# Linear attention and a gated feed-forward block on one core: group 1's output stage by seven block products, with the plan around it set anew

## The chip, the core and the metric

The kernel runs on one core of a Trainium2 chip. A core has five engines that run side by side and meet at semaphores: TensorE (PE; its weight loads are shown apart as PEld), VectorE (DVE), ScalarE (ACT), GpSimd (POOL) and SyncE (SP). DMAs are issued by SP, ACT or POOL. The metric is the device time of one execution in microseconds (us); of several executions the median counts.

## What is computed

```python
# q, k, v: [8 batches, 8 heads, 576 positions, 64]; cos_w, sin_w by position
def phi(x, c, s):
    r = np.maximum(x, 0.0)
    return np.concatenate([r * c, r * s], axis=-1)
kv  = einsum('bhsf,bhsd->bhfd', phi(k), v)
z   = sum(phi(k), axis=2)
x   = einsum('bhsf,bhfd->bhsd', phi(q), kv) / (einsum('bhsf,bhf->bhs', phi(q), z) + 1e-6)
x   = x.transpose(0, 2, 1, 3).reshape(4608, 512)          # tokens by model width
g   = x @ w_gate                                          # w_gate, w_val: [512, 1536]
out = (g * sigmoid(g) * (x @ w_val)) @ w_out              # w_out: [1536, 512], all float32
```

## The kernel before

**Tiles, groups, slots.** The 4608 tokens are 36 tiles of 128, and 9 groups (`tg` 0 to 8) of four tiles. A group's feed-forward work has twelve blocks (`fc`) of 128 hidden columns: gate and value products (`ffn_mm`, L605), silu on ACT (L611), product of the two on DVE into `ht` (L616). Then comes an output stage: `ht` times `w_out` for four tiles. While group `tg` runs, the attention of the next group's tiles is computed in between.

The order of all work is written out by hand. `slot(n)` is called 16 times per group (`SLOTS`, 12 after the blocks and 4 in the output stage) and runs what `plan` holds for slot n: so slot 16 tg + i is place i of group tg. The tables at the top set the places: `ROW[b]` for batch b those of `phi_q` (relu on ACT, L277, times cos/sin on DVE, L294, into `r_q`), of the DMA transposes of `r_q` into `phit` (L323, on SP's queue), of relu of k and of `vmul` (DVE, L304), and of the `kv` product (L354) with its copies out (L380 or L386); `TILES[tg]` those of the attention tiles (`a_tile2`: product L485, then `x_of` on DVE: L499, L508, L512, then `x_turn`, a DMA transpose into `xT` on SP's queue, L589). `WSUM` places four sums of gate weights (L638).

**Products by seven.** Groups 5 to 8 (`GATE`) compute the gate, and groups 2 to 8 the output, by a Strassen-like scheme: the matrices are cut into 2 x 2 blocks, and seven block products with sums of blocks (`ffn_by_quarters`, L663 for the gate and L676 for the value; `out_by_quarters`, L839) stand for eight. The output stage needs sums of weight blocks T1 to T4 (`weight_sum`, L802, kept in `wt_sb`) and of token blocks S1 to S4 (`token_sum`, L811, called by `sums_behind` after blocks 7 to 11, and inside the stage). The seven products are 12 matmuls of 256 columns each, in the order a, e = S3 T3, b += S2 T2, a again, b += S1 T1, c, b += S4. Between them: ACT copies a to b (L861) and e to C22 (L864), DVE adds C22 to c (L869) and b to C22 (L880), ACT copies out C11 and C21 (L852), DVE C12 (L854). Groups 0 and 1 multiply directly (`ffn_out`, L780: per tile twelve matmuls of 512 columns, then one copy, L787 on ACT or L789 on DVE). The weight sums are made inside group 1's output stage, one after each tile.

**PSUM banks.** `take` gives the eight banks in order of last use. From group 5 on (`loose`) it goes by `used`, an estimate of when a bank's reader will be done, and takes the earliest; `KVONE` lists the batches whose kv takes two single banks instead of a neighbouring pair.

**Loads and stores.** q, k and v of a batch (576 KB of float32 each, cast on the way) are loaded on GpSimd's queue. `load_behind(b)` first waits with a tiny copy (`hold`, L1051) until `phit` of batch b - 1 has landed. With `AHEAD = 5` it loads for b = 3: q3; for 4: q4, k4, v4, q5; for 5: k5, v5, q6; for 6: k6, v6, q7; for 7: k7, v7. Output rows are collected in `ob` and stored by `store` (L762, per tile two stores of 64 rows), in groups 1 to 7 on GpSimd's queue; the last group stores half-columns of two tiles by `store_two` (L769) and of one by `store`, one half of the rows from SP and the other from ACT.

Of the kernel before, what the change touches and what calls it, by code (L numbers as in the profile page):

```python
# [18 lines left out]
def kernel(  # L19
# [10 lines left out]
    nc = tc.nc  # L30
# [19 lines left out]
    HD = d_model // 2  # L50
    KH = KC // 2
    GATE = (5, 6, 7, 8)
    AHEAD = 5
    WSUM = (29, 38, 48, 64)
    ROW = {2: ([16, 16, 17, 17], 18, (20, 21, 21, 22), 8), 3: ([12, 12, 13, 13], 18, (17, 20, 21, 21), 6), 4: ([12, 12, 14, 14], 14, (13, 16, 17, 18), 5), 5: ([12, 12, 12, 14], 14, (14, 16, 17, 17), 5), 6: ([6, 8, 11, 12], 12, (13, 14, 15, 18), 3), 7: ([6, 6, 7, 7, 8, 8, 9, 9, 10, 10, 11, 11, 12, 12, 13, 13, 14, 14], 16, (12, 13, 14, 15), 3)}
    TILES = {2: (2, 9, 10, 11), 3: (5, 8, 10, 11), 4: (5, 7, 9, 11), 5: (3, 4, 7, 9), 6: (0, 2, 5, 7), 7: (0, 1, 5, 7), 8: (0, 3, 5, 7)}
    KVONE = (2, 5)
    LATER = {2: (0, 1, 3, 4, 7, 8), 3: (0, 1, 3, 4, 7, 8), 4: (0, 1, 3, 4, 7, 8), 5: (0, 1, 3, 4, 7, 8), 6: (0, 1, 3, 4, 7, 8), 7: (0, 1, 3, 4, 7, 8), 8: (0, 1, 3, 4, 7, 8)}
    LATE = dict(M=44, V=87, O=131, X=26, x=150, v=(190, 250, 120, 150), e=130, a=90, c=170, b=110, k=120)

# [21 lines left out]

    filled = [False] * 8
    loose = [False]
    rows = [0]

    def take(n, hold=None, fills=False, seeded=False):

        taken = {x for r in held.values() for x in r}
        if loose[0]:  # L90
            free = [b for b in range(8) if b not in taken]
            if n == 1:
                bs = [min((b for b in free if filled[b] or not seeded), key=lambda b: used[b])]
            else:
                b0 = min((b for b in free if b + 1 in free), key=lambda b: max(used[b:b + 2]))
                bs = [b0, b0 + 1]
            if hold is not None:
                held[hold] = bs
            for b in bs:
                filled[b] = fills or seeded  # L100
            touch(bs)
            return banks[:, bs[0]] if n == 1 else banks[:, bs[0]:bs[0] + 2]
        free = [b for b in range(0, 8, n) if not any(b <= x < b + n for x in taken)
                and (filled[b] or not seeded)]

        b0 = min(free, key=lambda b: (n == 1 and hold is not None and hold[0] == "o" and b ^ 1 not in taken,
                                      sorted(used[b:b + n], reverse=True)))
        if hold is not None:
            held[hold] = range(b0, b0 + n)
# [655 lines left out]
    def store_two(t, cols):  # L765
        for e in range(2):
            (b, c), (b1, _) = divmod(2 * t + e, NC), divmod(2 * t + 2 + e, NC)
            assert b == b1
            (nc.sync, nc.scalar)[e].dma_start(  # L769
                out=out_v[b, c:c + 3:2, :, cols].rearrange("c p f -> p c f"),  # L770
                in_=obs[t // 2][e * SH:(e + 1) * SH, :, cols])

# [40 lines left out]
    def sums_behind(fc):  # L813
        for n, lo, hi in {7: ((3, 0, 4),), 8: ((1, 0, 4),), 9: ((2, 0, 4),), 10: ((4, 0, 4), (3, 4, 6)),
                          11: ((1, 4, 6), (2, 4, 6))}.get(fc, ()):
            token_sum(n, lo, hi)

    def out_by_quarters(tg, slot_of):

        last = tg == NTG - 1  # L820
        queues = (nc.gpsimd, nc.gpsimd) if tg > 0 else None
        t0 = tg * OUT
        for t in (t0, t0 + 2):
            ob_of(t)
        C11, C12 = (obs[t0 // 2][:, :, x * HD:(x + 1) * HD] for x in range(2))
        C21, C22 = (obs[t0 // 2 + 1][:, :, x * HD:(x + 1) * HD] for x in range(2))

        def home(nm, parts=1, **kw):
            return [take(1, ("o", tg, nm, i), **kw).rearrange("p (t x) -> p t x", x=HD) for i in range(parts)]

        def free(nm, parts=1):
            for i in range(parts):
                give_back(("o", tg, nm, i))

        def product(to, a, b, first):
            rows[0] += LATE["O"]
            for kc in range(HC):
                for i in range(2):
                    nc.tensor.matmul(out=to[i][:, 0] if len(to) == 2 else to[0][:, i],  # L839
                                     lhsT=a[:, kc, i * P:(i + 1) * P], rhs=b[:, kc],  # L840
                                     start=first and kc == 0 and i == 0,
                                     stop=kc == HC - 1, skip_group_check=True)

        def each(ps, *others):
            if len(ps) == 1:
                return [(ps[0], *others)]
            return [(ps[i][:, 0:1], *(o[:, i:i + 1] for o in others)) for i in range(2)]

        def copied(eng, o, ps, x=DOWN):
            for p_, o_ in each(ps, o):  # L850
                if eng == "act":
                    nc.scalar.mul(out=o_, in_=p_, mul=x)  # L852
                else:
                    nc.vector.tensor_single_scalar(out=o_, in_=p_, scalar=x, op=ALU.mult)  # L854

        nb = 2 if last else 1
        a = home("a", fills=True)
        product(a, aq[:, 0, 0], bq[:, 0, 0], True)
        b = home("b", nb, seeded=True)
        for p_, o_ in each(b, a[0]):  # L860
            nc.scalar.copy(out=p_, in_=o_)  # L861
        e = home("e", fills=True)
        product(e, S3, T3, True)
        nc.scalar.mul(out=C22, in_=e[0], mul=DOWN)  # L864
        c = home("c", seeded=True)
        free("e")
# [12 lines left out]
        for p_, x_ in each(b, C22):  # L879
            nc.vector.scalar_tensor_tensor(out=x_, in0=p_, scalar=DOWN, in1=x_, op0=ALU.mult, op1=ALU.add)  # L880
        if last:
            store_two(t0 + 2, slice(HD, d_model))
        product(c, aq[:, 1, 1], T4, False)
        copied("act", C21, c)
        free("c")
        if last:
            store_two(t0 + 2, slice(0, HD))
        else:
            for t in (t0 + 2, t0 + 3):
                store(t, queues=queues)  # L890
        slot_of(2)
        product(b, S4, bq[:, 1, 1], False)
        copied("dve", C12, b)
        free("b", nb)
        for t in (t0, t0 + 1):
            store(t, *((slice(HD, d_model), (nc.sync, nc.scalar)) if last else (slice(0, d_model), queues)))
        slot_of(3)
# [41 lines left out]
    def turn(t, fast=False):  # L939
        return lambda: x_turn(t, fast)  # L940
# [83 lines left out]
    def load_2():  # L1024

        nc.gpsimd.tensor_copy(out=hold2, in_=xT[1][0:1, 0, 0, 0:2])
        for nm in ("k", "v"):
            load(2, nm)

    at((0, 1), turn(4), load_2)  # L1030
    at((1, 0), turn(5), a_(6, 0))
    at((1, 1), a_(6, 1))
# [70 lines left out]
    for tg in range(1, NTG):  # L1103
        s0 = SLOTS * tg
        if tg in GATE:
            if not loose[0]:
                loose[0] = True
                rows[0] = max(used) + 1
            ffn_by_quarters(tg, lambda i: slot(s0 + i))
        for fc in range(FC) if tg not in GATE else ():  # L1110
            ffn_fc(tg, fc)
            if tg > 1:
                sums_behind(fc)
            slot(s0 + fc)
        if tg > 1:
            out_by_quarters(tg, lambda i: slot(s0 + FC + i))
            continue
        for i in range(OUT):
            ffn_out(tg * OUT + i, queues=(nc.gpsimd, nc.gpsimd))
            weight_sum(i)  # L1120
            slot(s0 + FC + i)
    assert not plan, sorted(plan)


# [28 lines left out]
```

## Time and profile before

| | us |
|---|---|
| median of 4 runs (314.13 to 314.38) | 314.37 |
| the profiled execution | 314.13 |
| its span, first to last instruction | 312.3 |
| PE busy in the span | 304.0 |
| DVE / ACT / POOL busy | 235.9 / 154.3 / 66.6 |

The profile is of one execution. In a group of the page and in a timeline, a row is a line of the kernel on an engine, with its operation and tiles (out<-in); in a timeline the first two numbers are start and length in us from the span's start, x the number of merged instructions, and the bracket the idle time of the engine before it with what ended it. SPq, ACTq and POOLq are the queues on which DMAs are issued. The chain follows the work back from the last instruction, at each step to what released it.

### The profile page before, as it was taken

The page shows a single profiled execution, that of the slowest core. Times are in us where ns is not written, and L with a number is a line of the kernel's source. Part 1 is how long each engine was busy: PE and PEld are TensorE (multiplying, and loading weights), DVE is VectorE, ACT ScalarE, POOL GpSimd, SP SyncE. Part 2 cuts the span into 40 slices and gives each one's busy share as a digit, 9 for nine tenths or more (in the row PEclk, how much of TensorE's full clock was granted, in tenths as well). Part 3 has the DMA queues.
Part 4 walks back from the last instruction along what each step waited for, and adds up shares of the span by engine and source line. Part 5 has one row for each costly group of instructions (what it writes and reads, how often), then busy time and mean ns, then how long its engine had stood idle before and what let it go on. Part 6 is the DMA issues. An engine that isn't in the chain of part 4 may idle for free.

```text
span 312.3 us, 6945 instructions
## 1 busy us (share of the span) xinstructions
PE 304.0 (97%) x2768; PEld 197.2 (63%) x2768; DVE 235.9 (76%) x474; ACT 154.3 (49%) x294; POOL 66.6 (21%) x118
## 2 busy tenths in 40 slices
PE   8899999999999999999999999999999999999992
PEld 4587465445445486547654686778767877786682
DVE  7874778787876988587887987898789569855771
ACT  7454555673435346435545455788544344334520
POOL 7844202001522205030403031202200220040000
PEclk9999999999999999999999999999999999999998
DMA  7999998997797997979497989891980141022005
GB/s 265 221 198 197 207 204 125 237 140 101 119 242 114 168 189 108 170 108 190 96 188 81 201 130 150 117 158 21 178 138 20 25 129 36 20 66 68 2 1 134
DMA packets 72976, 41.08 MB, mean 132 GB/s; under 512 B 49904, under 2 KB 69872, under 8 KB 72944
## 3 DMA queue, kind: packets, MB, share of 16 engines
q0 software_dynamic: 24880, 24.91, 46.8%
q1 hardware_dynamic: 47472, 15.21, 31.2%
q10 hardware_dynamic: 592, 0.52, 0.6%
q8 instruction: 21, 0.34, 0.4%
q14 instruction: 11, 0.09, 0.1%
HBM read 37.75 MB, written 9.44 MB: 151 GB/s over the span
## 4 chain that ended last, share of the span: by engine, by line
PE 93%; DVE 3%; ACT 2%; issue 0%; DVEq 0%; ACTq 0%
PE banks L605 33%; PE banks L839 21%; PE banks L676 13%; PE banks L663 11%; PE banks L780 6%; PE banks L354 3%; PE banks L485 2%; PE banks L535 1%; PE banks L466 1%; DVE v L304 1%; DVE ht L681 1%; PE banks L208 1%; PE banks L577 0%; PE banks L409 0%; ACT L240 0%; DVE x L512 0%
## 5 line engine op out<-in xcount | busy, mean ns | idle before, releaser
L611 ACT ACTIVATE sg<-banks 128x512 bf16<-128x512 f32 (+2 forms) x68 | 37.1, 547 | 52.5 <-PE banks L605 51.8
L605 PE MATMUL banks<-xT,wg_sb 128*128 128x512 f16 (+2 forms) x272 | 62.0, 354 | 0.0
L605 PE MATMUL banks<-xT,wv_sb 128*128 128x512 f16 (+2 forms) x272 | 62.0, 354 | 0.0
L616 DVE TENSOR_TENSOR ht<-sg,banks 128x512 f16<-128x512 bf16 (+2 forms) x68 | 41.7, 621 | 21.9 <-PE banks L605 15.4
L762 POOL DMA_DIRECT2D out_dram<-ob x56 | 29.5, 534 | 118.1 <-ACT ob L852 112.3
L676 PE MATMUL banks<-xT,wv_sb 128*128 128x512 f16 x192 | 48.6, 379 | 0.0
L605 PEld LDWEIGHTS <-wv_sb 128*128 128x128 f16 x272 | 26.0, 98 | 26.1
L605 PEld LDWEIGHTS <-wg_sb 128*128 128x128 f16 x272 | 24.8, 98 | 21.5
L839 PEld LDWEIGHTS <-ht 128*128 128x128 f16 x336 | 32.7, 98 | 4.8
L681 DVE TENSOR_TENSOR ht<-sg,banks 128x512 f16<-128x512 bf16 x48 | 31.0, 681 | 3.3 <-ACT sg L669 3.3
L676 PEld LDWEIGHTS <-wv_sb 128*128 128x128 f16 x192 | 18.8, 98 | 13.3
L839 PEld LDWEIGHTS <-sums 128*128 128x128 f16 x252 | 24.6, 98 | 2.9
L669 ACT ACTIVATE sg<-banks 128x512 bf16<-128x512 f32 x36 | 20.5, 589 | 11.8 <-PE banks L663 11.8
L780 PE MATMUL banks<-wo_sb,ht 128*128 128x512 f16 x96 | 22.7, 379 | 0.0
L512 DVE TENSOR_TENSOR x<-banks,rec 128x512 f16<-128x512 f32 (+1 forms) x32 | 21.6, 674 | 1.3 <-PE banks L466 0.3
L663 PEld LDWEIGHTS <-wgs_sb 128*128 128x128 f16 x192 | 17.8, 98 | 7.4 <-issue 0.6
L663 PE MATMUL banks<-kvt,wgs_sb 128*128 128x256 f16 x144 | 21.6, 273 | 0.4 <-DVE x L512 0.4
L839 PE MATMUL banks<-wo_sb,ht 128*128 128x256 f16 x168 | 20.6, 273 | 0.0
L304 DVE TENSOR_TENSOR v<-raw_v,tab 128x1152 bf16<-128x1152 bf16 x27 | 19.8, 752 | 0.3 <-ACT raw_v L902 0.3
L839 PE MATMUL banks<-wt_sb,sums 128*128 128x256 f16 x168 | 19.5, 273 | 0.0
L839 PE MATMUL banks<-wt_sb,ht 128*128 128x256 f16 x168 | 19.5, 272 | 0.0
L852 ACT ACTIVATE ob<-banks 128x512 f32<-128x512 f32 x14 | 8.4, 597 | 22.2 <-PE banks L839 22.2
(125 smaller groups left out, 410.4 us busy)
## 6 DMA issues: line engine op xcount, KB each, us to landing
out_dram<-ob POOLq DMA_DIRECT2D x56, 128.0 KB, 4.5
raw_k<-in_k_dram POOLq DMA_DIRECT2D x7, 576.0 KB, 6.2
raw_q<-in_q_dram POOLq DMA_DIRECT2D x6, 576.0 KB, 11.4
raw_v<-in_v_dram POOLq DMA_DIRECT2D x6, 576.0 KB, 9.7
wo_sb<-in_moe_w_out_dram POOLq DMA_DIRECT2D x3, 512.0 KB, 12.8
out_dram<-ob SPq DMA_DIRECT2D x11, 128.0 KB, 5.5
wg_sb<-in_moe_w_gate_dram POOLq DMA_DIRECT2D x5, 256.0 KB, 9.8
wv_sb<-in_moe_w_val_dram POOLq DMA_DIRECT2D x5, 256.0 KB, 10.1
```

What stands on the lines that cost most here:

```text
L304: nc.vector.tensor_tensor(out=v2s[b == 1][:, g, :, :, 0:D], in0=(first if b == 0 and g == 0 else {"v": raw_of(b, "v")})["v"][:, g].unsquee ...
L512: nc.vector.tensor_tensor(out=st["x", t].rearrange("p (y e d) -> p e y d", e=2, d=D)[:, :, ys], in0=ps[:, :, 0:2 * J * D1].rearrange("p e ...
L605: nc.tensor.matmul(out=st["f", tg, fc, lo][i], lhsT=(wg_sb, wv_sb)[i][:, kc, fs], rhs=xT[tg][:, ts, kc], start=(kc == 0), stop=(kc == KC - 1))
L611: nc.scalar.activation(out=sg[:, 0:n], in_=st["f", tg, fc, lo][0], func=AF.Silu, scale=DOWN)
L616: nc.vector.tensor_tensor(out=ht[:, fc, r:r + n], in0=st.pop(("s", tg, fc, lo))[:, 0:n], in1=ps[1], op=ALU.mult)
L663: nc.tensor.matmul(out=to[:, i], lhsT=a[:, c, 2 * u + i], rhs=x[:, :, c], start=first and i == 0 and c == 0, stop=c == KH - 1, skip_group_ ...
L669: nc.scalar.activation(out=gates[u, w][:, :, j * HT:(j + 1) * HT], in_=src, func=AF.Silu, scale=DOWN)
L676: nc.tensor.matmul(out=val[u, i, w], lhsT=wv_sb[:, kc, fc * P:(fc + 1) * P], rhs=xT[tg][:, :, kc], start=(kc == 0), stop=(kc == KC - 1))
L681: nc.vector.tensor_tensor(out=ht[:, fc], in0=gates[u, w][:, i], in1=val.pop((u, i, w)), op=ALU.mult)
L762: (queues or (nc.sync, nc.sync))[e].dma_start(out=out_v[idx // NC, idx % NC][:, cols], in_=ob_of(t)[e * SH:(e + 1) * SH, cols])
L780: nc.tensor.matmul(out=o_ps[t], lhsT=ht[:, fc, r:r + P], rhs=wo_sb[:, fc], start=(fc == 0), stop=(fc == FC - 1))
L839: nc.tensor.matmul(out=to[i][:, 0] if len(to) == 2 else to[0][:, i], lhsT=a[:, kc, i * P:(i + 1) * P], rhs=b[:, kc], start=first and kc == ...
```

## The change

- Group 1's output goes through `out_by_quarters` as well, with `sums_behind` in its blocks. The four weight sums move ahead of it (`TSUM`): to places 2 and 3 of the third part of group 0's output stage, and to slots 18 and 19 (blocks 2 and 3 of group 1).
- In the last group, `store_two` issues its second half on GpSimd's queue instead of ACT's (`store` of the last C12 halves stays on SP and ACT), and the last of the seven products (`halves`) does all six matmuls of its first half before those of its second.
- `take`, once `loose`, counts its calls, and at the calls listed in `SECOND` gives the second choice.
- `AHEAD` 5 to 6 (q5 is loaded by `load_behind(5)`, ahead of k5 and v5, instead of by `load_behind(4)`), `KVONE` gets batch 4, one entry of `WSUM` and several of `ROW` and `TILES` move by one or two slots (`TILES[2][0]` is not used).

```diff
-    AHEAD = 5
-    WSUM = (29, 38, 48, 64)
-    ROW = {... 3: ([12, 12, 13, 13], 18, (17, 20, 21, 21), 6), 4: ([12, 12, 14, 14], 14, (13, 16, 17, 18), 5), 5: ([12, 12, 12, 14], 14, (14, 16, 17, 17), 5), ...}
-    TILES = {2: (2, 9, 10, 11), 3: (5, 8, 10, 11), ...}
-    KVONE = (2, 5)
+    AHEAD = 6
+    WSUM = (31, 38, 48, 64)
+    ROW = {... 3: ([12, 12, 14, 14], 18, (17, 20, 21, 21), 6), 4: ([12, 12, 12, 14], 14, (15, 16, 17, 18), 5), 5: ([12, 12, 12, 14], 15, (14, 16, 16, 17), 4), ...}
+    TILES = {2: (0, 9, 10, 11), 3: (5, 9, 10, 11), ...}
+    SECOND = (31, 37, 38, 79)
+    TSUM = [(2, 2), (2, 3), 18, 19]
+    KVONE = (2, 4, 5)
...
             free = [b for b in range(8) if b not in taken]
+            picks[0] += 1
+            other = picks[0] in SECOND
             if n == 1:
-                bs = [min((b for b in free if filled[b] or not seeded), key=lambda b: used[b])]
+                bs = sorted((b for b in free if filled[b] or not seeded), key=lambda b: used[b])
+                bs = bs[min(other, len(bs) - 1):][:1]
             else:
-                b0 = min((b for b in free if b + 1 in free), key=lambda b: max(used[b:b + 2]))
+                b0 = sorted((b for b in free if b + 1 in free), key=lambda b: max(used[b:b + 2]))
+                b0 = b0[min(other, len(b0) - 1)]
...
-            (nc.sync, nc.scalar)[e].dma_start(
+            (nc.sync, nc.gpsimd)[e].dma_start(
...
-        def product(to, a, b, first):
+        def product(to, a, b, first, halves=False):
             rows[0] += LATE["O"]
-            for kc in range(HC):
-                for i in range(2):
+            steps = [(kc, i) for kc in range(HC) for i in range(2)]
+            for kc, i in sorted(steps, key=lambda x: x[1]) if halves else steps:
...
-        product(b, S4, bq[:, 1, 1], False)
+        product(b, S4, bq[:, 1, 1], False, last)
...
+    for n in range(4):
+        at(TSUM[n], lambda n=n: weight_sum(n))
...
             ffn_fc(tg, fc)
-            if tg > 1:
-                sums_behind(fc)
+            sums_behind(fc)
             slot(s0 + fc)
-        if tg > 1:
-            out_by_quarters(tg, lambda i: slot(s0 + FC + i))
-            continue
-        for i in range(OUT):
-            ffn_out(tg * OUT + i, queues=(nc.gpsimd, nc.gpsimd))
-            weight_sum(i)
-            slot(s0 + FC + i)
+        out_by_quarters(tg, lambda i: slot(s0 + FC + i))
```

More of the change, by code (lines that the diff above doesn't have):

```diff
@@ L52 @@
     GATE = (5, 6, 7, 8)
-    AHEAD = 5
-    WSUM = (29, 38, 48, 64)
-    ROW = {2: ([16, 16, 17, 17], 18, (20, 21, 21, 22), 8), 3: ([12, 12, 13, 13], 18, (17, 20, 21, 21), 6), 4: ([12, 12, 14, 14], 14, (13, 16, 17, 18), 5), 5: ([12, 12, 12, 14], 14, (14, 16, 17, 17), 5), 6: ([6, 8, 11, 12], 12, (13, 14, 15, 18), 3), 7: ([6, 6, 7, 7, 8, 8, 9, 9, 10, 10, 11, 11, 12, 12, 13, 13, 14, 14], 16, (12, 13, 14, 15), 3)}
-    TILES = {2: (2, 9, 10, 11), 3: (5, 8, 10, 11), 4: (5, 7, 9, 11), 5: (3, 4, 7, 9), 6: (0, 2, 5, 7), 7: (0, 1, 5, 7), 8: (0, 3, 5, 7)}
-    KVONE = (2, 5)
+    AHEAD = 6
+    WSUM = (31, 38, 48, 64)
+    ROW = {2: ([16, 16, 17, 17], 18, (20, 21, 21, 22), 8), 3: ([12, 12, 14, 14], 18, (17, 20, 21, 21), 6), 4: ([12, 12, 12, 14], 14, (15, 16, 17, 18), 5), 5: ([12, 12, 12, 14], 15, (14, 16, 16, 17), 4), 6: ([6, 8, 11, 12], 12, (13, 14, 15, 18), 3), 7: ([6, 6, 7, 7, 8, 8, 9, 9, 10, 10, 11, 11, 12, 12, 13, 13, 14, 14], 16, (12, 13, 14, 15), 3)}
+    TILES = {2: (0, 9, 10, 11), 3: (5, 9, 10, 11), 4: (5, 7, 9, 11), 5: (3, 4, 7, 9), 6: (0, 2, 5, 7), 7: (0, 1, 5, 7), 8: (0, 3, 5, 7)}
+    SECOND = (31, 37, 38, 79)
+    TSUM = [(2, 2), (2, 3), 18, 19]
+    KVONE = (2, 4, 5)
     LATER = {2: (0, 1, 3, 4, 7, 8), 3: (0, 1, 3, 4, 7, 8), 4: (0, 1, 3, 4, 7, 8), 5: (0, 1, 3, 4, 7, 8), 6: (0, 1, 3, 4, 7, 8), 7: (0, 1, 3, 4, 7, 8), 8: (0, 1, 3, 4, 7, 8)}
@@ L84 @@
     loose = [False]
+    picks = [0]
     rows = [0]
@@ L833, in free @@
                 give_back(("o", tg, nm, i))
-        def product(to, a, b, first):
+        def product(to, a, b, first, halves=False):
             rows[0] += LATE["O"]
-            for kc in range(HC):
-                for i in range(2):
[L839 to L842, printed above, removed]
+            steps = [(kc, i) for kc in range(HC) for i in range(2)]
+            for kc, i in sorted(steps, key=lambda x: x[1]) if halves else steps:
+                nc.tensor.matmul(out=to[i][:, 0] if len(to) == 2 else to[0][:, i],
+                                 lhsT=a[:, kc, i * P:(i + 1) * P], rhs=b[:, kc],
+                                 start=first and kc == 0 and i == 0,
+                                 stop=kc == HC - 1, skip_group_check=True)
         def each(ps, *others):
```

## The prediction

> **What bounds the kernel now.** I read the page's busy shares and chain first, then the chain in order of time, then the timelines of the places that the diff touches. The page says that TensorE is the bound almost everywhere:
>
> ```profile
> PE 304.0 (97%) x2768; PEld 197.2 (63%) x2768; DVE 235.9 (76%) x474; ACT 154.3 (49%) x294; POOL 66.6 (21%) x118
> ...
> PE 93%; DVE 3%; ACT 2%; issue 0%; DVEq 0%; ACTq 0%
> ```
>
> So a change pays by taking matmul time away, by closing one of the few gaps, or behind the last matmul. The chain in order of time shows the output stage of group 1 (L780, 48 matmuls of 512 columns) and those of groups 2 and 3 (L839, 84 of 256 columns):
>
> ```profile
> 77.51 10.36 PE banks L780 x48
> ...
> 111.13 9.20 PE banks L839 x84
> ...
> 143.36 9.19 PE banks L839 x84
> ```
>
> Both run without gaps: 10.36/48 = 0.216 us and 9.19/84 = 0.109 us. The chain also names the only place after 20 us where other engines hold TensorE up for long, in group 5, between the a2 product (L485) and the kv product of batch 6 (L354):
>
> ```profile
> 190.45 0.27 PE banks L485 x8
> ...
> 191.26 0.69 DVE x L512
> 191.95 1.80 DVE ht L681 x3
> 193.75 0.04 issue
> 193.79 1.24 PE banks L354 x69
> ```
>
> Two stalls hide in it: a product (L663) waits until VectorE has read an a2 bank (L512), some 0.58 us; then L676, four matmuls from 192.44, ends at 192.44 + 4 x 0.216 = 193.30, and L354 starts at 193.79 when the third L681 has freed its bank: 0.49 us.
>
> The end, in the timeline (start, length, queue or engine):
>
> ```profile
> 303.37 4.43 SPq L769 DMA_DIRECT2D out_dram<-ob  x3
> 303.38 3.16 ACTq L769 DMA_DIRECT2D out_dram<-ob  x2
> ...
> 306.57 0.76 DVE L854 TENSOR_SCALAR ob<-banks 128x256 f32<-128x256 f32 x2 [1.86 <-PE banks L839]
> 306.58 0.60 ACT L852 ACTIVATE ob<-banks 128x512 f32<-128x512 f32 x1 [3.24 <-PE banks L839]
> 307.21 0.63 ACTq L769 DMA_DIRECT2D out_dram<-ob  x1
> 307.89 1.20 SPq L762 DMA_DIRECT2D out_dram<-ob  x2
> 307.94 1.44 ACTq L762 DMA_DIRECT2D out_dram<-ob  x2
> ```
>
> ScalarE copies C21 only at 306.58, though its product ended about 305.16: it was busy issuing stores. A narrower window (302 to 305) splits them:
>
> ```profile
> 303.38 2.44 ACTq L769 DMA_DIRECT2D out_dram<-ob  x1
> ```
>
> ScalarE's first store takes 2.44 us to issue, SP's at the same moment 0.65, ScalarE's later ones 0.56 to 0.79. It is the first DMA that ScalarE issues in this program. ScalarE's last issue starts at 308.82, lands 2.2 later at 311.0, and the span ends at 312.3.
>
> **What the Trainium skill says.** "TensorE: Matmul & The Clock Gate", Back-to-back issue gap: a warm matmul takes N/2.4 + 2.5 ns from start to start, 216 and 109 ns for 512 and 256 columns; the trace agrees (above). "DMA: Bandwidth & Descriptors", Issuing engines are not separate DMA queues: stores from any engine run on the same 16 DMA engines, so another issuer saves only sequencer time. The trace shows that this is not always small: 2.44 us. Same page, Latency and other measured facts: first byte about 0.6 us by the hardware path, 1 us by GpSimd's. Here landings hardly differ: group 7's eight GpSimd stores took 2.2 to 3.1 us, ScalarE's last two 2.2 and 2.6. No page prices a first DMA of an engine.
>
> **The change, part by part** (against the profiled execution: 314.13 us, span 312.3, so 1.8 around it; the median is 314.37, 0.24 more).
>
> 1. *Group 1's output, seven products.* Removed 48 x 0.216 = 10.36, added 84 x 0.109 = 9.19: **-1.17 us**, all on the path. It adds token sums on VectorE: three of 128x1024 into `sums` and one into `ht` (0.6 each at the pitch of the timeline), four of 128x512 (0.35 to 0.45), some 4 us; weight sums (4 x 0.95) leave the stage and go to slots with idle before L616 (0.6 and 1.0 around 61 to 63 us) and to group 0's output, where L789 becomes 0.6 late but its bank isn't wanted for long. I walked the new VectorE order from 68.56 with these pitches: the last-but-one `x` (L512) ends near 78.5, S2's second part near 80.0, the last `x` near 81.0. TensorE wants them at 78.66 (77.35 + 1.31; the second product takes that a2 bank), 80.8 (S2's last two blocks) and 81.3 (L869). So it fits, by 0.1, 0.8 and 0.3 us. Waiting behind VectorE there are the last token turn (SP, wanted 86.5; issued 81.1, 2.4 to 4.2 us) and group 2's first L616. Bounds of a stall: 0 to 0.6; I take 0. Stores of group 1 are now issued after both halves, 2 us later on GpSimd's queue; behind them is the `hold` of batch 4's loads, which sat idle 8.94 us before 99.7, waiting for `phit`. That turn itself starts about 1.5 us later (two phi products move to slot 30); q4 landed at 106.33 and is wanted at 114: covered.
> 2. *Group 5's kv bank.* In the built program's bank numbers the chooser now starts from a permuted state. kv takes two banks whose readers are a silu (done 192.1) and the first L681 (done 192.6), not the third: **-0.49**. The product before it still takes the a2 bank, at the same distance: 0.58 stays. The second choices (picks 31, 37, 38, 79) change no other distance to a last reader to under what ran without a stall before: 0; bounds -0.1 to +0.5.
> 3. *q5's load, one batch later.* Batch 5's query (576 KB) leaves group 2's loads and heads group 3's. Four loads in group 2 landed 6.0, 9.9, 13.8 and 17.3 us after 100.35; three in group 3 at 6.2, 10.0, 13.2 after 135.65. Token turns issued beside loads land only about when loads end: group 2's last two 0.6 and 1.0 after them, group 3's last 1.1. Group 3's loads wait for `phit` of batch 4, whose turn starts 2 us earlier (three of four phi products now at slot 44): loads at about 133.6, last landing 150.9, last turn 151.5. Group 4 starts at 152.55 - 1.17 = 151.4. **+0.2**; bounds 0 (turn lands with the pace of before) to 2.3 (below). q5 itself lands at 140 and is wanted at 146, v5 at 147.4 and at 150.
> 4. *kv of batch 4 in two single banks:* eight half casts for four, +0.3 on each of ACT and DVE; DVE idled 1.23 us before them: 0. kv of batch 5 one slot earlier: its v product is done at 158.5, wanted about 160: 0. Gate weight sum two slots later, tile 13 one slot later, phi and v slots: VectorE work moved within its slack: 0.
> 5. *The end.* Three stores go to GpSimd (issue 0.53 us; nothing queued behind). ScalarE copies C21 at 305.3. The last product runs its halves one after the other, so the first C12 copy starts 6 x 0.109 = 0.65 earlier (305.92) and ends at 306.34; the second still ends at 306.99, 0.34 before today's. SP then issues its last stores until 307.7, landing 309.5. But ScalarE's first DMA is now the first C12 store: 306.36 + 2.44 = 308.80, the next at 308.85, landing 311.05 against 311.0. **+0.05**. If the long issue doesn't come back: second store at 307.0, SP last, 309.5: -1.55. I take the first: the only thing that sets that issue apart in the trace is being ScalarE's first.
>
> Sum: 314.13 - 1.17 - 0.49 + 0.20 + 0.05 = 312.72; on the median's footing 312.96. I predict 312.9.
>
> **The rivals.**
> - *The end gets short.* The 2.44 us belonged to that moment (two engines issuing at once), not to a first use. For it: SP issued at the same instant. Against: at 307.2 both issued together again at 0.59 and 0.63. 312.96 - 1.6 = 311.3.
> - *The bank choice gives nothing, or VectorE is late in group 1 by as much:* 0.49 back: 313.4. For it: margins of 0.1 and 0.3 us in part 1.
> - *Group 4's tokens are late, change slower.* One mechanism: the last token turn before group 4 lies behind four loads. Under loads turns took 8.8 and 8.9 us (101.43, 107.41). At 8.9 the last, issued at 144.8, lands at 153.7, 2.3 after 151.4: 314.37 - 1.17 - 0.49 + 0.05 + 2.3 = 315.1. It decides from a stall of 1.6 on, and passes 0.2% at 2.2. In between, 1 to 2 us, it comes out even: 314.2. For it: DMA share is 0.93 already in 120 to 143 us. Against: the last turn of a group ran behind the load tail in both windows and took 4.0 and 4.4.
> - *The change doesn't do what it says:* the built order has the 84 matmuls in group 1, so I give it nothing.
>
> **How the numbers follow.** Forecast 0.55; short end 0.19; 0.5 lost 0.08; tokens late and even 0.09; tokens late and slower 0.09. Range: from the short end (311.3, with 0.1 below) to 313.9, which takes in one unexpected stall up to 1 us; left out are the two late cases, 0.18. A measurement of this kernel tells about 0.2% (0.63 us) from no change: faster 0.55 + 0.19 + 0.08 = 0.82, same 0.09, slower 0.09.
>
> **What would show it.** Group 1's output as L839-kind x84 of 9.2 us with no DVE piece in the chain beside it; kv in group 5 starting right after L676, the DVE `x` piece before it still there; group 4's first gate matmul within 0.3 us of the stage before it; ScalarE's first DMA in the end 2.4 us long and the last to land. I am wrong if that issue is 0.6 us long, if the chain shows a DMA of xT or DVE ahead of group 4, or if group 5's first stall is gone too.

## The result and the profile after

| | us |
|---|---|
| changed kernel, median of 39 executions (313.75 to 318.9) | 315.95 |
| kernel before, median of 59 beside it (313.64 to 314.83) | 314.09 |
| ratio, 95% interval | 1.0051 (1.0038 to 1.0064) |
| the profiled execution of the changed kernel, its span | 313.9, 312.1 |

The change makes the kernel slower by about half a per cent; 312.9 was predicted. The executions come in three bunches: 15 from 313.75 to 314.91, 17 from 315.88 to 316.77, 7 from 317.25 to 318.9. The profile is of the first bunch, so what sets the other two apart is not in it. In the changed kernel the line numbers of the places named here are 7 higher than before (L780 is L787, L839 is L846, the stores L762 and L769 are L769 and L776); the closing line L1148 is L1150.

The changed kernel's page, busy time and the chain by engine, against 304.0 us and 93% before:

```profile
PE 302.7 (97%) x2804; PEld 200.6 (64%) x2804; DVE 240.2 (77%) x485; ACT 155.8 (50%) x298; POOL 68.4 (22%) x121
...
PE 91%; DVE 5%; ACT 2%; issue 1%; DVEq 0%; ACTq 0%
```

TensorE has 1.3 us less to do. The changed kernel's chain in order of time (start, length, what), at the output stages of groups 1, 2 and 3 and the start of group 4:

```profile
77.63 9.17 PE banks L846 x84
...
110.06 9.19 PE banks L846 x84
...
142.28 9.19 PE banks L846 x84
151.47 6.91 PE banks L612 x32
```

Group 1's stage is now 84 short matmuls in 9.17 us, unbroken, where 48 long ones took 10.36. In this execution group 4 begins where group 3 ends. Its chain in group 5:

```profile
190.17 0.70 DVE x L519
190.87 0.04 issue
190.91 0.60 PE banks L670 x4
191.51 0.86 PE banks L683 x4
192.37 1.17 PE banks L361 x68
```

The wait for VectorE's `x` is still there; kv (L361) now starts when the four L683 end (191.51 + 0.86), so the wait of 0.49 is gone. So far all is as predicted: TensorE ends 1.49 us earlier (305.15 against 306.64). The end, in the changed kernel's timeline:

```profile
301.88 3.21 SPq L776 DMA_DIRECT2D out_dram<-ob  x3
302.15 0.61 POOL L776 DMA_DIRECT2D out_dram<-ob  x1 [21.91 <-ACT ob L859]
...
304.77 0.61 POOL L776 DMA_DIRECT2D out_dram<-ob  x1 [0.65 <-ACT ob L859]
304.99 3.25 ACTq L769 DMA_DIRECT2D out_dram<-ob  x2
305.19 1.20 SPq L769 DMA_DIRECT2D out_dram<-ob  x2
```

ScalarE's two stores take 3.25 us together, 2.61 of it the first; the last store lands at 309.70. Before, the last landed at 311.00 and the span ended 1.3 later, at 312.3. Here it ends 2.4 later. What fills that is in the rows of the kernel's closing line, which the chain doesn't show (count, shortest/median/longest in ns, first and last start). The changed kernel:

```profile
L1150 SPq EVENT_SEMAPHORE  x11: 17/28/1000, 306.4 to 312.1; - x11
L1150 POOLq EVENT_SEMAPHORE  x4: 17/17/17, 311.4 to 312.0; - x4
L1150 POOLq DRAIN  x3: 51/102/6577, 304.7 to 311.8; - x3
```

and the kernel before:

```profile
L1148 POOLq DRAIN  x3: 51/93/6733, 280.7 to 312.1; - x3
```

GpSimd's program closes with a DRAIN of 6.6 us that begins within half a microsecond of the issue of its last DMA. Before, that DMA was issued at 281.2 and the drain ran from 280.7 to 287.4. Now it starts with the last GpSimd store and runs from 304.75 to 311.33, while SyncE, which waits for all stores, is through at 309.97. The other engines then wait for GpSimd.

### The profile page after: what moved, and what is told of

Read it like the earlier page. It is cut to its first block, busy times and chain, and to the rows that moved or that the text cites. A ratio compares the mean times of both kernels' runs of the same rounds, so it can differ in the third digit from the quotient of the medians.

```text
span 312.1 us, 7025 instructions
## 1 busy us (share of the span) xinstructions
PE 302.7 (97%) x2804; PEld 200.6 (64%) x2804; DVE 240.2 (77%) x485; ACT 155.8 (50%) x298; POOL 68.4 (22%) x121
## 4 chain that ended last, share of the span: by engine, by line
PE 91%; DVE 5%; ACT 2%; issue 1%; DVEq 0%; ACTq 0%
PE banks L612 31%; PE banks L846 24%; PE banks L683 13%; PE banks L670 12%; PE banks L787 3%; PE banks L492 2%; PE banks L361 2%; DVE v L311 1%; PE banks L542 1%; PE banks L473 1%; PE banks L215 1%; DVE ht L623 1%; PE banks L416 0%; PE banks L584 0%; ACT L247 0%
## 5 line engine op out<-in xcount | busy, mean ns | idle before, releaser
L769 POOL DMA_DIRECT2D out_dram<-ob x56 | 29.4, 534 | 116.6 <-ACT ob L859 115.0
L683 PE MATMUL banks<-xT,wv_sb 128*128 128x512 f16 x192 | 48.6, 379 | 0.0
L846 PEld LDWEIGHTS <-ht 128*128 128x128 f16 x384 | 37.4, 98 | 5.3
L846 PEld LDWEIGHTS <-sums 128*128 128x128 f16 x288 | 28.2, 98 | 3.3
L683 PEld LDWEIGHTS <-wv_sb 128*128 128x128 f16 x192 | 18.8, 98 | 13.3
L846 PE MATMUL banks<-wo_sb,ht 128*128 128x256 f16 x192 | 23.6, 273 | 0.0
L846 PE MATMUL banks<-wt_sb,ht 128*128 128x256 f16 x192 | 22.3, 273 | 0.0
L846 PE MATMUL banks<-wt_sb,sums 128*128 128x256 f16 x192 | 22.3, 273 | 0.0
L859 ACT ACTIVATE ob<-banks 128x512 f32<-128x512 f32 x16 | 9.6, 597 | 23.9 <-PE banks L846 23.9
L301 DVE TENSOR_TENSOR r_q<-raw_q,tab 128x1152 bf16<-128x1152 bf16 x20 | 14.4, 752 | 5.2 <-ACT raw_q L284 4.7
```

The lines of the kernel that those rows point to most:

```text
L301: nc.vector.tensor_tensor(out=st[b, "q"][:, g], in0=o.unsqueeze(2).to_broadcast([P, NC, 2, D]), in1=tab, op=ALU.mult)
L683: nc.tensor.matmul(out=val[u, i, w], lhsT=wv_sb[:, kc, fc * P:(fc + 1) * P], rhs=xT[tg][:, :, kc], start=(kc == 0), stop=(kc == KC - 1))
L769: (queues or (nc.sync, nc.sync))[e].dma_start(out=out_v[idx // NC, idx % NC][:, cols], in_=ob_of(t)[e * SH:(e + 1) * SH, cols])
```

## The experiments

The theory after this look was that the closing drain makes both the loss and the spread. Against it stood that the loss and the spread come from the earlier parts of the change, and that stores over GpSimd's queue might be slow as such. Each median below stands against the kernel before, run in the same rounds (313.95 to 314.11).

### The last group's stores

`tail_back` is the change with ScalarE's queue put back; `tail_alone` is the kernel before with GpSimd's put in:

```diff
-            (nc.sync, nc.gpsimd)[e].dma_start(
+            (nc.sync, nc.scalar)[e].dma_start(
```

> The changed kernel with the last group's second halves issued by ScalarE again, everything else as changed. Drain theory (GpSimd's closing DRAIN runs some 6.6 us from its last DMA and ends the program): GpSimd's last DMA is then at about 280 us, the drain is hidden, and the time is that of the last landing: 312.4 to 312.9, with the narrow spread of the kernel before (about 1 us over all runs). Rival (the spread and the loss come from the earlier parts of the change: group 1's sums, the loads, the banks): the median stays near 315.9 and the spread at some 5 us.

> The kernel before with nothing changed but the second halves of the last group's paired stores on GpSimd's queue. Drain theory: last GpSimd DMA at about 306.3, drain to 312.9, span about 313.6 in the profile, and in timed runs as much above the kernel before as the change is above its own landing time, so 316.5 to 317.5 with a spread of several us. Rival (the loss is in the earlier parts): 314.1 and as narrow as before.

`tail_alone`: 315.25, narrow (315.06 to 315.84), ratio 1.0040 (1.0027 to 1.0053): slower by 1.26 with nothing else changed. Its closing line:

```profile
L1148 POOLq DRAIN  x3: 51/93/6577, 306.2 to 313.2; - x3
```

The drain has the same 6577 ns. The stores had all landed by 309.83, 1.2 before those of the kernel before, and the drain then takes 2.6 us more. GpSimd's queue need not be what shortens the stores: ScalarE's first one is no longer long here (0.57), and two kernels below that keep ScalarE's queue and lose only that long store end as early, 3.52 and 3.53 us from TensorE's last matmul to the last landing against 3.53 here. `tail_back`: 313.66, spread over 311.32 to 316.1; ratio 0.9981 (0.9961 to 1.0002). So the drain is one cause, and the spread isn't of its making. That part of the theory failed in both runs: without the drain the run was to be narrow and is wide, and with it alone it was to be wide, at 316.5 to 317.5, and is narrow.

Two more keep GpSimd out in part or wholly, by naming the second queue of each of the three `store_two` calls: `pool_once` GpSimd, SyncE, SyncE; `act_first` ScalarE, SyncE, ScalarE.

```diff
-    def store_two(t, cols):
+    def store_two(t, cols, second):
...
-            (nc.sync, nc.gpsimd)[e].dma_start(
+            (nc.sync, second)[e].dma_start(
```

> The changed kernel with only the first of the three paired stores (C11, issued near 302.2) on GpSimd, the other two on SP for both halves. Drain theory, fixed length from the last DMA: the drain ends 2.6 us earlier than in the changed kernel, at about 308.7, before the last landing plus closing: span about 311.0, time 312.8 and narrow. If instead the drain waits until the DMA rings are quiet, or is long in any way as soon as GpSimd issued a DMA near the end: it stays at 313.5 to 316 and wide. First-use theory of ScalarE: its first DMA is still the first C12 store and takes 2.4 us or more.

> The changed kernel with no GpSimd store in the last group: first paired store on SP and ScalarE, second on SP alone, third on SP and ScalarE. ScalarE's slow first DMA (2.4 us) then falls at about 302 to 304.3, beside the remaining products, and its last ones take 0.6. Drain theory and first-use theory together: last landing at about 308.5, span about 309.8, time 311.6 and narrow. If the slow issue is not a first use but comes with the end: 312.8. If the loss is in the earlier parts: near 315.

`pool_once` 313.64 (311.75 to 315.9), `act_first` 314.58 (311.34 to 316.09): again wide, where narrow runs were expected, in bunches near 311.4 to 312, 313.6 and 315.4. What is left is the prediction's rival "group 4's tokens are late". Their profiles, unlike that of the change, fell in the upper bunches and show why. `act_first`, timeline:

```profile
144.96 1.20 SPq L596 DMA_TRANSPOSE xT<-x  x1
...
153.31 0.55 PEld L612 LDWEIGHTS <-wg_sb 128*128 128x128 f16 x4 [2.32 <-DMA xT<-x]
153.32 1.04 PE L612 MATMUL banks<-xT,wg_sb 128*128 128x512 f16 x4 [2.04 <-DMA xT<-x]
```

The last token turn is issued at 144.96, as early as in the profile of the change (145.15), but lands 8.3 us later instead of 5.2, and TensorE's first gate product of group 4 waits for it. The start is 2.21 us later than an unbroken one, 1.95 in `pool_once`, 2.27 in `tail_back`. In `act_first` and `tail_back` something comes on top. `act_first` by stretches (length; busy time and count of PE, PEld, DVE, ACT and POOL; mean granted TensorE clock, 1.00 being full speed; DMA share, GB/s):

```profile
145.00:151.00 6.00, 6.00 (x57) 5.34 (x55) 3.63 (x6) 3.67 (x7) 0.13 (x1) 1.00 1.24 193
151.00:153.30 2.30, 0.28 (x3) 0.00 (x0) 2.03 (x3) 0.72 (x2) 1.99 (x4) 1.00 0.93 143
153.30:158.00 4.70, 4.68 (x14) 1.78 (x15) 1.83 (x3) 1.94 (x4) 2.08 (x4) 0.64 0.98 170
158.00:163.00 5.00, 5.00 (x31) 2.40 (x30) 3.79 (x8) 2.17 (x4) 0.00 (x0) 1.00 1.10 197
```

In the stretch after the gap the mean granted clock is 0.64: the first five matmuls of 512 columns follow each other at full pace, and then eight at 0.427 us instead of 0.216, another 1.7 us. In `pool_once` there are none. No wait, a wait of 2, and a wait of 2 with a slow stretch make the three bunches. For the change itself, whose upper bunches no profile caught, this reading is carried over from these kernels.

### q5's load

```diff
-    AHEAD = 6
+    AHEAD = 5
```

(A batch's query is 1152 KB as float32 and 576 KB as it lands.) The edit is made in `act5` on `act_first`, in `drain_only` on the change with nothing else undone; `before6` has the reverse edit on the kernel before.

> The change with q5's load back in group 4 (AHEAD 5) and with the last group's stores kept off GpSimd's queue (ScalarE's, SyncE's, ScalarE's). If the loss has two causes, the late token turn of group 4 and GpSimd's closing drain, both are gone: a narrow run at 311.4 (the lowest cluster of tail_back and act_first, 311.3 to 311.7), 2.6 below the kernel before. If group 4's turn is late for another reason than q5's load, the spread of 311.4 to 316 stays, with the median near 313.6.

> The change with AHEAD 5 and nothing else undone, so all of the last group's second stores stay on GpSimd's queue. If q5's load is what makes group 4 late, no wait for the tokens before group 4 and a narrow run; the drain at the end stays, worth 1.3 (tail_alone against the kernel before): 311.4 plus 1.3 to 2.5, so 312.7 to 313.9, where 313.9 is the changed kernel's own execution without the wait. If the spread comes from the stores' queue, it stays 313.7 to 318.9 with a median of 315.9.

> The kernel before with one edit, AHEAD 6 (q5's load moved from group 4 to group 3). The step as predicted: the last token turn of group 4 lands at 151.5, TensorE wants it at 152.4, so no wait and 314.1. The late-turn theory: the turn comes behind four loads, takes 8 us and lands at 153.0 to 154.0; TensorE, 1.2 us later here than in the changed kernel, waits 0.5 to 1.5: 314.6 to 315.6 in those executions, 314.1 in the others, so a wider run with a median of 314.3 to 315.3.

| | median | lowest to highest, executions | ratio to before (95%) |
|---|---|---|---|
| act5 | 311.82 | 311.56 to 312.26, 5 | 0.9931 (0.9919 to 0.9943) |
| drain_only | 314.06 | 313.69 to 315.45, 22 | 1.0003 (0.9993 to 1.0013) |
| before6 | 315.12 | 314.86 to 318.21, 11 | 1.0047 (1.0029 to 1.0066) |

With the load back in group 2 the two upper bunches are gone in both kernels (three of the 22 of `drain_only` still lie at 315.1 to 315.45): from `drain_only` to the change it costs 1.89, from `act5` to `act_first` 2.76, alone on the kernel before 1.17. (In `before6` TensorE gets to group 4 at 152.4, 0.9 later than in the change; its profiled execution, at 316.43 the second longest of the eleven, waits 2.43 there.) And `drain_only` less `act5`, 2.24, is what the change's queues cost at the end: in the profiles the last landing comes 0.85 later (309.61 against 308.76, with ScalarE's long store in it), and the drain adds the rest. `act5` beats the kernel before by 0.69%; no other version here does better. In `act5` the last turn into `xT` before group 4 lands 3.5 us after its issue (last line):

```profile
L596 SPq DMA_TRANSPOSE xT<-x x1: 1189/1189/1189, 145.3 to 145.3; - x1
...
DMA to landing us min/median/max: 3.5/3.5/3.5
```

The load's old place isn't free either. TensorE now reaches group 3 about 1.2 us sooner, and there the last turn lies behind the four loads of group 2. In the kernel before it landed at 118.67, 1.5 ahead of TensorE; `act5`, chain in order of time, at the start of group 3:

```profile
113.03 6.08 DMA xT<-x
119.12 0.14 issue
119.25 0.81 PE banks L612 x3
```

TensorE waits 0.32 there, in `act5_whole` (below) 0.40, and in the profile of `act5_nosecond` (below) 1.32, where the loads ended later (119.51 against 118.20 in `act5`). With three loads in group 2, in the change, that turn lands at 115.66. So the change's move of q5's load relieves group 3 and loads group 4; the prediction weighed only group 4.

Is it q5 at the head of the list, or the fourth load in group 3's window? `act9` keeps q5's load in group 3 but loads every later query with its own batch (AHEAD = B), so the window holds q5, k5, v5 and not q6.

> act_first with AHEAD = B: every batch's query is loaded with its own keys and values, so group 3's window has three loads (q5, k5, v5) where act_first has four (q5, k5, v5, q6). If the number of loads ahead of the last token turn makes group 4 late, no wait before group 4 and a narrow run at 311.5 to 312.3, as act5. If q5's load at the head of the list does it (it delays k5 and v5), the wait of about 2 stays: a median of 313.5 to 315, as act_first.

At group 4 there was no wait: the turn, issued at 145.12, landed at 149.12. The loads started when those of `act_first` did (135.15 and 135.08), and the last of three landed at 148.27 where the last of four landed at 153.00. So it is the number of loads ahead of the turn. With four, their start goes with the outcome: 133.23 in the profile of the change, which didn't wait, and 134.35 to 135.10 in the three that did; what one profile against three can't show is that nothing else differs. The time itself went to 328.41 (ratio 1.0444, 1.0405 to 1.0483): the missing look-ahead is paid in groups 4 and 5, where TensorE stands for 6.2 and 6.1 us, and runs at half the granted clock for a while after. `act9`, chain in order of time, at the first of them:

```profile
167.55 5.67 DMA raw_q<-in_q_dram
173.22 0.02 issue
173.24 0.69 ACT raw_q L284
...
176.26 0.70 DVE x L519
176.96 0.04 issue
177.00 0.60 PE banks L492 x8
```

q6, now issued at 167.55, is wanted at once: ScalarE stands at its relu until 173.22, and all that is queued behind it and behind VectorE's product with it, TensorE's next `x` included, stands too. The expected 311.5 to 312.3 was wrong for the whole and right for the place it was about.

Last, `pool_first5` asks what of GpSimd's queue costs: `drain_only` with only the first of three stores left on it.

> drain_only with two of the last group's three GpSimd stores on SyncE's queue instead; GpSimd keeps the first. If the loss is a closing drain of some 6.5 us after GpSimd's last store, it ends here near 309, with SyncE's closing waits, and costs nothing: 311.6 to 312.2, narrow. If stores over GpSimd's queue are slow as such, one of them still costs about a third of the 2.2: 312.5 or more.

312.14 (311.72 to 316.31, 22 executions; all but the highest under 313.3), ratio 0.9945 (0.9930 to 0.9960). Its closing line:

```profile
L1150 POOLq DRAIN  x3: 51/93/6418, 302.2 to 309.8; - x3
```

The drain is as long, but is over at 302.19 + 6.42 = 308.61, before the last landing at 309.11. So the drain costs nothing here, where GpSimd's last store is 6.9 us ahead of the last landing. The 0.3 between this median and that of `act5` has the size of the difference in their last landings (309.11 and 308.76); ScalarE's first store takes 1.94 us here.

### Group 1's seven products alone, and the tables

`group1_alone` is the kernel before with `out_by_quarters` in group 1, `TSUM` and the first `WSUM` entry; `group1_rows` adds `ROW` and `TILES` of the change, `group1_tables` also `KVONE`:

```diff
+    TSUM = [(2, 2), (2, 3), 18, 19]
-    KVONE = (2, 5)
+    KVONE = (2, 4, 5)
...
-            if tg > 1:
-                sums_behind(fc)
+            sums_behind(fc)
...
+        out_by_quarters(tg, lambda i: slot(s0 + FC + i))
```

`act5_nosecond` is `act5` with `SECOND = ()`, `act5_tables` is that with `ROW`, `TILES` and `KVONE` of before, `act5_whole` is `act5` without the order by halves in the last product.

> The kernel before with group 1's output by seven products and the weight sums ahead of it, nothing else. By part 1's working TensorE gains 1.17 and no stall is added: 314.0 less 1.17, less the 0.12 by which group 1 starts later for the sums: 312.8 to 313.0. If the work around it (VectorE's combinations in group 1, the a2 product's wait of 0.21 that the changed kernel shows in group 2) takes it back, 313.2 to 313.8.

> group1_alone with ROW and TILES of the change. If the query's phi products on VectorE (0.68 each, at L295) in group 1's output stage are what holds TensorE up there, moving two of them to slot 30 takes the wait of 0.86 at 85 us away: about 313.0. Group 5's wait for the kv bank (0.49) stays. If the wait only moves, 313.9 as group1_alone.

> group1_rows with KVONE of the change too (batch 4's kv in two single banks). If KVONE is what takes group 5's wait of 0.49 away, 0.4 to 0.5 below group1_rows: about 312.5, close to act5_nosecond (312.36), from which it differs only in the last group's queues and order. If it does nothing, as group1_rows.

> As act5, with SECOND empty: every bank by first choice. If the second choices at 31, 37, 38 and 79 are what took group 5's wait for the kv bank away (0.49 us), this is 0.5 above act5, 311.9, with a wait of 0.3 to 0.6 on TensorE before L361 of group 5. If they do nothing, it equals act5 within 0.2.

> act5_nosecond with ROW, TILES and KVONE of the kernel before. If those moves do nothing on the path, as part 4 of the prediction has it, 312.4 as act5_nosecond (312.36). If they carry part of the gain, or take group 5's stall or group 2's away, 312.6 to 313.2.

> act5 without the order by halves in the last product (the two row blocks alternate again). The first C12 copy then waits for the whole product instead of its first four matmuls: its start comes up to 0.43 (four matmuls of 256 columns at 0.107) later, the last copy's does not. If the last store hangs on the last copy, nothing: 311.8. If it hangs on the queue of stores behind the first copy, 312.0 to 312.3.

| | median | ratio to before (95%) | waits of TensorE in the profile, beside two that all have |
|---|---|---|---|
| group1_alone | 313.91 | 0.9995 (0.9985 to 1.0006) | 0.86 in group 1; 0.49 in group 5; 0.25 in group 6; 0.59 in group 7 |
| group1_rows | 313.69 | 0.9991 (0.9981 to 1.0000) | 0.34 in group 5; 0.44 in group 6; 0.47 in group 7 |
| group1_tables | 312.49 | 0.9954 (0.9941 to 0.9967) | 0.59 in group 7 |
| act5_tables | 313.99 | 1.0006 (0.9994 to 1.0017) | 0.86 in group 1; 0.49 in group 5; 0.59 in group 7 |
| act5_nosecond | 312.36 | 0.9952 (0.9939 to 0.9964) | 1.32 in group 3; 0.59 in group 7 |
| act5 | 311.82 | 0.9931 (0.9919 to 0.9943) | 0.32 in group 3 |
| act5_whole | 312.01 | 0.9931 (0.9919 to 0.9943) | 0.40 in group 3; 0.52 in group 5 |

The two that all have are some 0.2 at 73 us and 0.5 to 0.6 before a product of group 5; waits under 0.1 are left out. Alone, group 1's products give nothing that can be measured, where 312.8 to 313.0, or 313.8 at most, was expected. `group1_alone`, timeline:

```profile
82.42 2.92 DVE L295 TENSOR_TENSOR r_q<-raw_q,tab 128x1152 bf16<-128x1152 bf16 x4
...
85.26 0.68 DVE L881 SCALAR_TENSOR_TENSOR ob<-banks,ob 128x512 f32<-128x512 f32 x1
86.00 1.25 PE L840 MATMUL banks<-wo_sb,sums 128*128 128x256 f16 x10 [0.70 <-DVE ob L881]
```

and the changed kernel at the same place:

```profile
82.61 1.42 DVE L301 TENSOR_TENSOR r_q<-raw_q,tab 128x1152 bf16<-128x1152 bf16 x2
...
84.22 0.69 DVE L887 SCALAR_TENSOR_TENSOR ob<-banks,ob 128x512 f32<-128x512 f32 x1 [0.18 <-PE banks L846]
85.32 1.47 PE L846 MATMUL banks<-wo_sb,sums 128*128 128x256 f16 x12
```

Four query products of 0.73 us stand on VectorE ahead of the addition into C12 that frees the bank for the last product. With the change's rows there are two, and the addition is done 1.04 earlier. The wait in group 1 goes with `ROW` and `TILES`; but by them alone (`group1_rows`) only 0.2 is gained, within the noise, where 0.9 was expected, as the kv product waits for banks in group 5 and anew in 6. With `KVONE` both are gone, and the time is 1.62 below before: the 1.17 of the stage and the 0.49 of group 5. `KVONE` without the rows was not run. The second choices take the wait of 0.59 in group 7 away (the expectation had looked for it in group 5); the time between the medians, 0.54, has that size, though the two intervals overlap. `act5_tables` shows the tables' share from the other side: without them all of the gain of `act5_nosecond` is gone, 1.63 between the medians, where 0 to 0.8 was expected. The order by halves shows no difference.

### ScalarE's long first store

The trace lists every instruction on ScalarE, waits too. In the kernel before the long store is the 447th listed after the first, and an instruction packet of 8 KB appears 0.38 us into it. `before_pad` issues the one-column Silu at the start, with which ScalarE loads its table, three times in a row instead of once; `late_pad` adds two such Silus in slots 40 and 41, `late_pad5` five in slot 40:

```diff
+    for s in range(5):
+        at(40, lambda: nc.scalar.activation(out=tiny, in_=half_pi, func=AF.Silu))
```

> The kernel before with the one-column Silu that loads ScalarE's table issued three times instead of once, at the start, so that everything after it stands two instructions later on ScalarE. If the slow first store of ScalarE (2.44 us at L769, the 447th instruction that the trace lists on ScalarE) belongs to its place in ScalarE's instruction stream, where the trace shows an instruction packet, the store takes 0.55 to 0.80 here and the end comes up to 1.5 earlier: 312.4 to 313.4. If the first DMA that ScalarE issues is slow as such, it stays at 2.4 and the time at 314.0. The store alone, 0.57 where tail_alone moved it to place 449, speaks for the first.

> The kernel before with two one-column Silus more on ScalarE, in slots 40 and 41 in the middle of the program, where ScalarE idles. before_pad showed ScalarE's first store at 0.74 instead of 2.44 and the end 1.1 shorter behind TensorE, but paid 0.86 for its two Silus at the start. Here the start stays: if the store's length belongs to its place, 0.55 to 0.80 at L769 and 1.0 to 1.5 less: 312.5 to 313.1. If the gain of before_pad's end was only its later TensorE, 314.0.

> The kernel before with five one-column Silus one after the other in slot 40. If ScalarE's slow issue belongs to place 447 of its stream, the first store, moved to a place after it, takes 0.55 to 0.80, and without before_pad's 0.86 at the start the end comes about 1.0 earlier: 312.8 to 313.3. If the place has nothing to do with it, 2.2 to 2.4 and 314.1.

The first store of `before_pad` (two lines further down there), of `late_pad` and of `late_pad5`, timelines:

```profile
304.25 0.74 ACTq L771 DMA_DIRECT2D out_dram<-ob  x1
```

```profile
303.32 2.20 ACTq L769 DMA_DIRECT2D out_dram<-ob  x1
```

```profile
303.91 0.74 ACTq L769 DMA_DIRECT2D out_dram<-ob  x1
```

`late_pad` failed to move the store: two waiting instructions fell away for the two added, it stayed at place 447, and stayed long (314.15, ratio 1.0004, 0.9995 to 1.0012). The other two moved it to 449 and it was short. In `before_pad` the end comes 1.1 sooner behind TensorE (3.53 from TensorE's last matmul to the last landing, 4.63 before), but TensorE is 0.8 later from the start on: 313.95, ratio 1.0002 (0.9991 to 1.0013). `late_pad5` doesn't pay that: 313.36, ratio 0.9976 (0.9966 to 0.9985).

Over all twenty kernels here: where ScalarE's first store stands at place 447 it takes 1.94 to 2.61 us (seven kernels), at 443 to 446, 449 and 451 it takes 0.57 to 0.74 (thirteen). In the seven, an instruction packet starts 0.26 to 0.93 us into the store. In the others it comes at some other time, in `act5` beside a later store that isn't long, so a packet as such doesn't make one long. The place is shown; that ScalarE waits there for its instructions is only argued.

## Why the prediction was wrong

- *Part 1, group 1's products, -1.17, no stall:* right in the change (9.17 us, no VectorE piece in the chain there). But the margin on VectorE exists only with the moves of `ROW` and `TILES`. In part 4 those and the other small moves were worth 0. What they do on the kernel before, without group 1's products, was not run; with these products they are what makes part 1 come out. The prediction missed 0.21 us at 73 us, where an a2 product waits for kv copies.
- *Part 2, kv bank of group 5, -0.49:* right in size and in what stays. The reason was half the truth: the order of banks that group 1's products leave isn't enough (`group1_alone` still waits 0.49), with the rows 0.34 stays, and only with `KVONE` too is the wait gone. The second choices, put at 0, are worth some 0.5, since all five kernels with group 1's products and without the second choices wait anew in group 7.
- *Part 3, q5's load, +0.2:* this failed, at the step "loads at about 133.6, last landing 150.9, last turn 151.5" with TensorE there at 151.4. The loads follow the landing of batch 4's `phit`. Its turn did start earlier, by 3 us and not 2 (124.0 to 124.3 against 127.24), but then took 8.3 to 10.4 us where it had taken 7.7 before. So the loads started at 133.23 in the profile of the change and at 134.35 to 135.10 in the three that caught the other case. Their length, taken as 17.3, was 16.7 to 18.0, and the turn's distance behind them, taken as 0.6, was 0.3 to 1.9. The turn landed at 150.36 in the first and at 153.0 to 153.4 in the three. The rival "group 4's tokens are late" had the mechanism and the size (8.9 us and 2.3 of wait; measured 8.1 to 8.4 and 1.95 to 2.27). It was held unlikely since the last turn ran behind the loads' tail and took 4.0 and 4.4 before. It runs behind the tail here too, but in the three the tail lies at 151.1 to 153.1, where TensorE wants the turn at about 151.1. The step should have asked for the spread: `phit` landed at 132.6 to 134.5 in four kernels with this order. Why its turn takes 8 us in one execution and 10 in another stays open.
- *Part 4, small moves, 0:* see part 1.
- *Part 5, the end, +0.05:* this failed too, at "nothing queued behind" for GpSimd's stores, with which the last landing was to end the program. The closing drain was queued there, and it ended the program. Without it the step fits: 311.05 less 1.46 is 309.59 for the last landing, 309.70 was measured. The drain ends 1.36 after SyncE's waits, and the profiled execution is at 313.9 where the sum was 312.72. That ScalarE's first store would again be long was right for this kernel, for a reason that is wrong: being the first doesn't do it. That the store kept place 447, with other instructions ahead of it, was luck.

Together: 312.72, and 1.2 for the drain, gives the profiled 313.9; what is left to the median, 2.05, is of the size of the wait for the turn. The Trainium skill's "DMA: Bandwidth & Descriptors", Issuing engines are not separate DMA queues, says that another issuing engine saves only sequencer time. The runs agree: the stores of `tail_alone` land 1.2 earlier, as much as ScalarE's queue gains where its one long issue is gone (`before_pad`, `late_pad5`). They add a cost on GpSimd's queue, at the end of the program, of which that section says nothing.

## What to carry to other kernels

Before moving the last DMAs to another queue, look at the rows of the closing line: what each engine does after its last work is on nobody's chain until it becomes the last thing. A step put at 0.1 late with bounds of "0 to 2.3" may come out either way in each execution, and one profile shows one side of it. When a stage gets shorter, look again at every later transfer that had a margin of about as much: here the last turns ahead of groups 3 and 4. A faster stage is worth its time only with the cover that its neighbours need: the same 1.17 us was nothing or all, by where two query products and a kv bank stood.

## What was not expected of the hardware

- GpSimd's closing DRAIN takes 6.42 to 6.73 us in all twenty kernels. It begins within half a microsecond of the issue of GpSimd's last DMA, whether that is at 280 us with 30 us to go or in the last 10. The Trainium skill's "VectorE: DVE Perf Modes", The DRAIN you can't avoid, has drains of some 12 ns on all five engines from what the runtime puts at a program's start and end. In this program's closing line only SyncE's are of that size (7 to 13 ns); the longest there are 0.40 us on ScalarE, 0.46 to 0.69 on VectorE, 1.85 to 1.92 on TensorE, and GpSimd's.
- ScalarE's store at one place in its instruction stream takes 1.94 to 2.61 us instead of 0.57 to 0.74; two places further on (`before_pad`, `late_pad5`) it is short.
- TensorE's granted clock is half for 3.41 us, which is eight matmuls, after a wait of 2.21 and of 2.27 us (`act_first`, `tail_back`), and stays whole after 1.95 and 2.43 (`pool_once`, `before6`). The half stretch starts 0.9 and 0.06 us after the restart. Up to it the traces record full clock for 44 and 43 times 3.413 us, and in the other two for 89 and 90 times that, past TensorE's last matmul. Cut into steps of this length, the two traces with the slow stretch have TensorE's whole idle time (2.04 and 2.11 us) inside one step; in the two without it a border of a step splits it (0.74 and 1.04, 1.39 and 0.88 us). So in these four it is the wait's place and not its length that decides. The Trainium skill's "TensorE: Matmul & The Clock Gate", What's actually happening, has the clock fall after an idle window of about 3.4 us that runs free of the program. The length and the free running agree; that 2.04 us of idle time in a window can do it is shorter than the page has it.
